# Linear attention and an MLP mixer on one core: from pairs of batches to single batches in a software pipeline

## The chip, the cores and the metric

The kernel runs on one core of a Trainium2 chip. A core has five engines, each with its own instruction queue, worked off in program order: TensorE (PE; its weight loads are shown apart as PEld), VectorE (DVE), ScalarE (ACT), GpSimd (POOL) and SyncE (SP). Here SP only issues transfers. POOL issues the transfers that load weights and cast them to bf16 on the way. Matmuls write to PSUM, which has eight banks of 2 KB a partition; VectorE and ScalarE read it from there.

The metric is the device time of one execution in microseconds, as the median of several runs. Beside it stands one profiled execution, whose trace is read here.

## The reference

For 8 batches, 8 heads, 576 positions and head size 64, a linear attention, then a mixer over positions (tokens) and one over channels:

```python
phi = lambda x: np.where(x > 0, x, np.exp(x) - 1.0) + 1.0
q_p, k_p = phi(q), phi(k)
kv  = einsum('bhsd,bhse->bhde', k_p, v);  z = sum(k_p, axis=2)
num = einsum('bhsd,bhde->bhse', q_p, kv)
den = einsum('bhsd,bhd->bhs', q_p, z)[..., None] + 1e-06
x   = (num / den), heads side by side: (8, 576, 512)
xt  = x.transpose(0, 2, 1)
h   = np.maximum(xt @ w_tok1, 0.0) @ w_tok2       # 576 -> 256 -> 576
u   = x + h.transpose(0, 2, 1)
h2  = np.maximum(u @ w_ch1, 0.0) @ w_ch2          # 512 -> 1536 -> 512
out = u + h2
```

Inputs and output are fp32; the matmuls run in bf16.

## The kernel before

The 576 positions of a batch are four row tiles of 128 (the position is `4p + r`, r = 0 to 3) and a tail of 64. The batches go in four pairs, and the two tails of a pair fill one tile of 128, so that a pair has nine row tiles.

For each batch, in this order:

- **phi** (L114 to L137): a chunk is four heads, 128 x 1024. ScalarE takes exp (L116), VectorE adds 1 (y, L117), takes the minimum of exp and 1 (e, L118), and the maximum of both (L126). The tail has the same steps at half the size (L136).
- **vcast** (L140 to L146): VectorE casts v to bf16 beside a column of ones, which gives z with the same matmul.
- **kv** (L148 to L159): for each of four head pairs, five matmuls of 130 columns (four row tiles and the tail), and ScalarE copies the result to kvbd.
- **qtr** (L161 to L181): TensorE transposes phi(q), ScalarE copies it to qT.
- **nd** (L183 to L200): for each row tile, four matmuls give numerators and denominators in a PSUM tile of two banks, of which there is one buffer. VectorE adds eps (L194), takes the reciprocal (L196) and multiplies (x, L198).
- **mm1** (L203 to L210) and **mm2** (L212 to L223): token mixing. mm1 has two column tiles of five matmuls of 512 columns, evicted with relu by ScalarE. mm2 has two such matmuls for each row tile; VectorE adds x and writes u (L222, and L220 for the tail).
- **utr** (L225 to L233): u transposed into uT.

Then the channel mixing for the pair. **mm3** (L236 to L245) goes over twelve column tiles; each has a group of four matmuls of 512 columns for each of the two batches (L239), evicted with relu by ScalarE (L243), and one of 128 columns for the tails, evicted by VectorE (L245). **mm4** (`slot_4`, L256 to L276) takes nine row tiles, each twelve matmuls of 512 columns in three parts of four, after which VectorE adds u (L266) and SP stores the tile.

The order is written by hand (`manual_schedule`). The first pair starts batch by batch: the whole attention and token mixing of batch 0, mm3 of batch 0 (`slot_a` twelve times), attention and token mixing of batch 1, the rest of mm3. Then, for each pair, the slots of mm3 (24) and mm4 (27) run in order, and a plan puts steps of the next pair behind given slots (`pos`, `ks`, `qs`). phi of k and vcast for the pair after next stand near or behind the last slots, phi of q for the next pair in its first slots.

PSUM has three pools: `ps_big` (three buffers of one bank, for mm3 and mm4), `ps_sm` (three of one bank, for all else) and `ps_nd` (one of two banks). The transfers of the first pair and of the weights are ordered by dependencies on earlier ones (`after`): an instruction waits on its issuing engine until the other transfer has landed, and what stands behind it on that engine waits too. Weights are issued by POOL, all else by SP. w2 is loaded in rows of its own order (w2raw) and rearranged by VectorE (L327, L330).

Of the kernel before, what the change touches and what calls it, by code (L numbers as in the profile page):

```python
# [9 lines left out]
FP32 = mybir.dt.float32  # L10
# [8 lines left out]
def kernel(  # L19
# [30 lines left out]
    work = ctx.enter_context(tc.tile_pool(name="work", bufs=2))  # L50
    outp = ctx.enter_context(tc.tile_pool(name="outp", bufs=3))
    ps_big = ctx.enter_context(tc.tile_pool(name="ps_big", bufs=3, space=bass.MemoryType.PSUM))
    ps_sm = ctx.enter_context(tc.tile_pool(name="ps_sm", bufs=3, space=bass.MemoryType.PSUM))
    ps_nd = ctx.enter_context(tc.tile_pool(name="ps_nd", bufs=1, space=bass.MemoryType.PSUM))
# [30 lines left out]
    u = [const(f"u{i}", [128, 9, DM]) for i in range(2)]  # L85
    uT = const("uT", [128, NDM, 9 * 128])
    cr = const("cr", [128, NCH, 9 * 128])
# [13 lines left out]
    def load_chunk(nm, p, b, g):  # L101
        hs = slice(4 * g, 4 * g + 4)
        s = src[nm][2 * p + b, hs, 0:SM, :].rearrange("h (p r) d -> p h (r d)", r=R)
        return nc.sync.dma_start(out=raw[nm, b][:, hs].rearrange("p h r d -> p h (r d)"), in_=s)
# [8 lines left out]
    def phi_flat(src_flat, dst, n):  # L113
        e = work.tile([128, 1024], BF16, name="e", tag="e")[:, :n]  # L114
        y = work.tile([128, 1024], BF16, name="y", tag="y")[:, :n]
        nc.scalar.activation(out=e, in_=src_flat, func=AF.Exp)  # L116
        nc.vector.tensor_scalar(out=y, in0=src_flat, scalar1=1.0, scalar2=None, op0=ALU.add)  # L117
        nc.vector.tensor_scalar(out=e, in0=e, scalar1=1.0, scalar2=None, op0=ALU.min)  # L118
        dst(e, y)

    def phi(nm, b, g):
        dstt = (kp if nm == "k" else qp)[b]
        f = raw[nm, b][:, 4 * g:4 * g + 4].rearrange("p h r d -> p (h r d)")
# [16 lines left out]
    def vcast(b, g):  # L140
        nc.vector.tensor_copy(out=vs[b][:, :, 4 * g:4 * g + 4, 0:D].transpose([0, 2, 1, 3]),  # L141
                              in_=raw["v", b][:, 4 * g:4 * g + 4])

    def vcast_tail():
        for b in range(2):
            nc.vector.tensor_copy(out=vst[b][half[b], :, 0:D], in_=raw["v", "t"][half[b]])  # L146

    def kv(b, g):  # L148
        ps = ps_sm.tile([128, 2, 256], FP32, name="kv_ps", tag="sm")
        for jj in range(2):  # L150
            j = 2 * g + jj
            for r in range(R):
                nc.tensor.matmul(out=ps[:, jj, 0:2 * D1], lhsT=kp[b][:, r, 2 * j:2 * j + 2, :],  # L153
                                 rhs=vs[b][:, r, 2 * j:2 * j + 2, :], start=(r == 0), stop=False)
            nc.tensor.matmul(out=ps[:, jj, 0:2 * D1], lhsT=kpt[:, 2 * j:2 * j + 2, :],  # L155
                             rhs=vst[b][:, 2 * j:2 * j + 2, :], start=False, stop=True)
        for i in range(2):
            nc.scalar.copy(out=kvbd[b][half[i], 2 * g:2 * g + 2, i * D1:(i + 1) * D1],
                           in_=ps[half[i], :, i * D1:(i + 1) * D1])  # L159

    def qtr(b, g):  # L161
        tp = ps_sm.tile([128, 8, 128], BF16, name="tp", tag="sm")
        for jj in range(2):
            for r in range(R):
                j = 2 * g + jj
                nc.tensor.transpose(  # L166
                    out=tp[:, jj * R + r, :],
                    in_=qp[b][:, r, 2 * j:2 * j + 2, :].rearrange("p a b -> p (a b)"),
                    identity=identity)
        nc.scalar.copy(out=qT[b][:, 2 * g:2 * g + 2].rearrange("p j r c -> p (j r) c"), in_=tp)  # L170

    def qtr_tail():
        tp = ps_sm.tile([128, 8, 128], BF16, name="tp", tag="sm")
# [8 lines left out]
    def nd(b, r):  # L182
        tail = r == R  # L183
        ps = ps_nd.tile([128, 2, 2, 256], FP32, name="nd_ps", tag="nd")
        for j in range(HP):
            nc.tensor.matmul(out=ps[:, j // 2, j % 2, 0:2 * D1],  # L186
# [3 lines left out]
        n = 64 if tail else 128  # L190
        v_ = ps.rearrange("p a b c -> p (a b) c")[ps_, :, 0:2 * D1]
        v_ = v_.rearrange("p j (h e) -> p j h e", h=2)
# [7 lines left out]
            in1=den[:, :, :, None].to_broadcast([n, HP, 2, D]), op=ALU.mult)  # L200


    def mm1(b, mt):  # L203
        ps = ps_sm.tile([128, DM], FP32, name="a_ps", tag="sm")
        ms = slice(128 * mt, 128 * mt + 128)
        for r in range(R):
            nc.tensor.matmul(out=ps, lhsT=w1[:, r, ms], rhs=x[b][:, r, :],  # L207
                             start=(r == 0), stop=False)
        nc.tensor.matmul(out=ps, lhsT=w1t[:, b, ms], rhs=xt, start=False, stop=True)  # L209
        nc.scalar.activation(out=ar[b][:, mt, :], in_=ps, func=AF.Relu)  # L210

    def mm2(p, b, r):  # L212
        tail = r == R
        ps = ps_sm.tile([128, DM], FP32, name="h_ps", tag="sm")
        for kt in range(NT):
            nc.tensor.matmul(out=ps, lhsT=w2t[:, kt, b, :] if tail else w2[:, kt, r, :],  # L216
                             rhs=ar[b][:, kt, :], start=(kt == 0), stop=(kt == NT - 1))
        if tail:
            h = half[b]
            nc.vector.tensor_tensor(out=u[p % 2][h, 8, :], in0=ps[h], in1=xt[h], op=ALU.add)  # L220
        else:
            nc.vector.tensor_tensor(out=u[p % 2][:, 4 * b + r, :], in0=ps, in1=x[b][:, r, :],  # L222
                                    op=ALU.add)  # L223

    def utr(p, t0, n):  # L225
        tp = ps_sm.tile([128, NDM, 2, 128], BF16, name="tp", tag="sm")
        for i in range(n):
            for j in range(NDM):
                nc.tensor.transpose(out=tp[:, j, i, :],  # L229
                                    in_=u[p % 2][:, t0 + i, 128 * j:128 * j + 128],  # L230
                                    identity=identity)
        dst = uT[:, :, 128 * t0:128 * (t0 + n)].rearrange("p j (i c) -> p j i c", i=n)
        nc.scalar.copy(out=dst, in_=tp[:, :, 0:n, :])  # L233


    def mm3_group(mc, c0, n, on_act=True):  # L236
        ps = ps_big.tile([128, 512], FP32, name="c_ps", tag="big")[:, :n]
        for kj in range(NDM):
            nc.tensor.matmul(out=ps, lhsT=wc1[:, kj, 128 * mc:128 * mc + 128],  # L239
                             rhs=uT[:, kj, c0:c0 + n], start=(kj == 0), stop=(kj == NDM - 1))  # L240
        dst = cr[:, mc, c0:c0 + n]
        if on_act:
            nc.scalar.activation(out=dst, in_=ps, func=AF.Relu)  # L243
        else:
            nc.vector.tensor_scalar(out=dst, in0=ps, scalar1=0.0, scalar2=None, op0=ALU.max)  # L245

    def slot_a(mc):
        mm3_group(mc, 0, 512)

    def slot_b(mc):  # L250
        mm3_group(mc, 512, 512)
        mm3_group(mc, 1024, 128, on_act=False)
# [3 lines left out]
    def slot_4(p, t, part):  # L256
        if part == 0:
            held["h2"] = ps_big.tile([128, DM], FP32, name="h2_ps", tag="big")
        ps = held["h2"]
        for kc in range(4 * part, 4 * part + 4):  # L260
            nc.tensor.matmul(out=ps, lhsT=cr[:, kc, 128 * t:128 * t + 128], rhs=wc2[:, kc, :],  # L261
                             start=(kc == 0), stop=(kc == NCH - 1))
# [3 lines left out]
        nc.vector.tensor_tensor(out=o, in0=ps, in1=u[p % 2][:, t, :], op=ALU.add)  # L266
        if t < 8:
            b, r = divmod(t, 4)
# [5 lines left out]


    parts = [(b, g) for b in range(2) for g in range(2)]  # L276
    landed = {}
    for nm, g in (("k", 0), ("v", 0), ("k", 1), ("v", 1)):
        landed[nm, g] = load_chunk(nm, 0, 0, g)
    load_tail("k", 0)  # L280
    load_tail("v", 0)
    landed["q", 0] = load_chunk("q", 0, 0, 0)
    load_chunk("q", 0, 0, 1)
# [4 lines left out]
    after(nc.gpsimd.dma_start(out=w1, in_=moe_w_tok1[0:SM, :].rearrange("(p r) t -> p r t", r=R)),  # L288
          landed["q", 0])
    for b in range(2):  # L290
        nc.gpsimd.dma_start(out=w1t[half[b], b, :], in_=moe_w_tok1[SM:S, :])
    nc.gpsimd.dma_start(out=w2raw, in_=moe_w_tok2.rearrange("(k p) s -> p k s", p=128))
    NB = 4
    CB = DCH // NB
    wc1_in = []
    for i in range(NB):
        cs = slice(CB * i, CB * (i + 1))
        wc1_in.append(nc.gpsimd.dma_start(
            out=wc1[:, :, cs], in_=moe_w_ch1[:, cs].rearrange("(k p) c -> p k c", p=128)))

# [7 lines left out]
    nc.vector.memset(w2t, 0.0)  # L308

    def next_k(b, g):  # L310
        if b == "t":
            phi_tail("k")
            vcast_tail()
        else:
            phi("k", b, g)
            vcast(b, g)

    for g in range(2):
        next_k(0, g)
    next_k("t", 0)  # L320
    kv(0, 0)
    kv(0, 1)
# [3 lines left out]
    for kt in range(NT):  # L326
        nc.vector.tensor_copy(out=w2[:, kt],  # L327
                              in_=w2raw[:, kt, 0:SM].rearrange("k (p r) -> k r p", r=R))
        for b in range(2):
            nc.vector.tensor_copy(out=w2t[:, kt, b, 64 * b:64 * b + 64], in_=w2raw[:, kt, SM:S])  # L330
    qtr(0, 0)
    qtr(0, 1)
# [3 lines left out]
    for mt in range(NT):  # L336
        mm1(0, mt)
    for r in range(R + 1):
        mm2(0, 0, r)
        if r in (2, 4):  # L340
            utr(0, r - 2, 2)

    gate = wc1_in[NB - 2]
    for nm in "kv":
        for g in range(2):
            landed[nm, 1, g] = after(load_chunk(nm, 0, 1, g), gate)
# [166 lines left out]
```

## Time and profile before

| | |
|---|---|
| median of 3 runs | 361.17 us (360.92 to 362.2) |
| the profiled execution | 359.34 us |
| its span, first to last instruction | 357.5 us |
| mean granted TensorE clock | 0.942 |
| TensorE matmul, busy | 280.5 us (78%) |
| TensorE weight loads | 148.2 us (41%) |
| VectorE | 185.4 us (52%) |
| ScalarE | 147.2 us (41%) |
| GpSimd | 10.0 us (3%) |
| read from and written to memory | 35.85 and 9.44 MB |

In the rows that follow, a group of instructions has its line, engine, operation, the tiles that it writes and reads, shapes and count; behind the bar stand its busy time in us, the mean of one in ns, and the idle time of the engine before it, with what ended it. In the timeline, a row starts with its start and its length in us from the start of the span. A row of waits has the waiting instruction, what it waited for, the total in us, how often, and the longest. In the 40 slices, each digit is a tenth of the busy share of 8.9 us, and PEclk is the granted clock in tenths. In a table by stage, the numbers behind the stretch are its length and the busy time of each engine, with the number of instructions in brackets.

### The profile page before, as it was taken

How to read it: one execution, taken by the hardware profiler on the slowest of the kernel's cores; microseconds unless marked ns; L12 is line 12 of the kernel's file. 1: busy time of each engine (PE TensorE's matmuls, PEld its weight loads, DVE VectorE, ACT ScalarE, POOL GpSimd, SP SyncE). 2: the span in 40 equal slices, each digit the busy share in tenths (PEclk: the TensorE clock that was granted, in tenths of full speed). 3: DMA queues.
4: the chain of work that ended last, by engine and by line, in shares of the span. 5: the costliest groups of instructions: out<-in, count | busy, mean ns of one | idle time of the engine just before them, and what ended most of it. 6: DMA issues, size and time to landing. Idle time of an engine off the chain costs nothing.

```text
span 357.5 us, 4635 instructions
## 1 busy us (share of the span) xinstructions
PE 280.5 (78%) x1776; PEld 148.2 (41%) x1776; DVE 185.4 (52%) x406; ACT 147.2 (41%) x229; POOL 10.0 (3%) x19
## 2 busy tenths in 40 slices
PE   0256864389949659808989999939889999999995
PEld 0133423135536324405544455426445454455442
DVE  6574325442599663698575362787571642211221
ACT  3431564135647202556944325239635121366000
POOL 1320300000000000000000000000000000000000
PEclk9999995589987999977999999989999999999999
DMA  7999959940299900169900022110000122100232
GB/s 251 220 180 294 244 152 272 289 109 0 65 297 302 280 29 30 61 202 315 274 2 3 0 61 88 60 61 0 2 0 2 29 88 90 60 0 2 65 114 88
DMA packets 47574, 41.82 MB, mean 117 GB/s; under 512 B 14272, under 2 KB 42816, under 8 KB 47552
## 3 DMA queue, kind: packets, MB, share of 16 engines
q1 hardware_dynamic: 43264, 37.76, 35.9%
q0 software_dynamic: 4288, 3.77, 6.8%
q8 instruction: 14, 0.23, 0.3%
q14 instruction: 8, 0.07, 0.1%
HBM read 35.85 MB, written 9.44 MB: 127 GB/s over the span
## 4 chain that ended last, share of the span: by engine, by line
PE 64%; DVE 23%; ACT 6%; issue 3%; DMA 2%; SPq 1%; ACTq 0%
PE h_ps L261 22%; PE c_ps L239 21%; DVE x L198 6%; PE nd_ps L186 5%; PE a_ps L207 4%; PE h_ps L216 4%; DVE y L117 3%; PE kv_ps L153 3%; DVE vs L141 2%; DMA k_rawt<-in_k_dram 2%; DVE e L118 2%; PE tp L229 2%; DVE kp L126 2%; DVE den L196 2%; ACT e L116 2%
## 5 line engine op out<-in xcount | busy, mean ns | idle before, releaser
L239 PE MATMUL c_ps<-uT,wc 128*128 128x512 bf16 (+1 forms) x576 | 103.8, 330 | 1.7 <-ACT uT L233 1.6
L261 PE MATMUL h_ps<-wc,cr 128*128 128x512 bf16 x432 | 101.8, 381 | 0.0
L243 ACT ACTIVATE cr<-c_ps 128x512 bf16<-128x512 f32 x96 | 57.8, 604 | 49.7 <-PE c_ps L239 49.5
L239 PEld LDWEIGHTS <-wc 128*128 128x128 bf16 x576 | 49.9, 99 | 45.8 <-issue 4.6
L261 PEld LDWEIGHTS <-cr 128*128 128x128 bf16 x432 | 41.3, 98 | 45.7 <-issue 1.2
L266 DVE TENSOR_TENSOR o_sb<-h_ps,u 128x512 f32<-128x512 f32 x36 | 24.8, 690 | 41.7 <-PE h_ps L261 41.7
L245 DVE TENSOR_SCALAR cr<-c_ps 128x128 bf16<-128x128 f32 x48 | 14.0, 291 | 53.4 <-PE c_ps L239 53.4
L233 ACT COPY uT<-tp 128x1024 bf16<-128x1024 bf16 (+1 forms) x20 | 18.2, 928 | 42.1 <-PE tp L229 42.0
L222 DVE TENSOR_TENSOR u<-h_ps,x 128x512 bf16<-128x512 f32 x32 | 21.3, 686 | 20.0 <-PE h_ps L216 19.9
L186 PE MATMUL nd_ps<-kvbd,qT 128*128 128x130 bf16 x128 | 15.1, 244 | 17.0 <-DVE x L198 13.0
L210 ACT ACTIVATE ar<-a_ps 128x512 bf16<-128x512 f32 x16 | 9.6, 597 | 45.4 <-PE a_ps L209 45.4
L118 DVE TENSOR_SCALAR e<-e 128x1024 bf16<-128x1024 bf16 (+1 forms) x40 | 16.0, 401 | 22.5 <-ACT e L116 22.2
L153 PE MATMUL kv_ps<-vs,kp 128*128 128x130 bf16 x128 | 15.2, 270 | 15.5 <-DVE vs L141 15.5
L155 PE MATMUL kv_ps<-vst,kpt 128*128 128x130 bf16 x32 | 8.7, 273 | 23.6 <-DVE vst L146 23.6
L198 DVE TENSOR_TENSOR x<-nd_ps,den 128x512 bf16<-128x512 f32 x32 | 22.1, 691 | 1.1
L116 ACT ACTIVATE e<-k_raw 128x1024 bf16<-128x1024 f32 x16 | 16.5, 1056 | 14.3 <-DVE kp L126 9.2
L153 PEld LDWEIGHTS <-kp 128*128 128x128 bf16 x128 | 12.0, 124 | 19.0 <-DVE kp L126 10.3
L186 PEld LDWEIGHTS <-qT 128*128 128x128 bf16 x128 | 8.6, 106 | 26.2 <-DVE x L198 21.3
L216 PE MATMUL h_ps<-ar,w 128*128 128x512 bf16 x64 | 18.1, 379 | 0.9 <-ACT ar L210 0.9
L116 ACT ACTIVATE e<-q_raw 128x1024 bf16<-128x1024 f32 x16 | 16.6, 1052 | 5.2 <-DVE kp L126 3.9
L170 ACT COPY qT<-tp 128x1024 bf16<-128x1024 bf16 x16 | 16.6, 1035 | 5.1 <-PE tp L166 5.1
L207 PE MATMUL a_ps<-x,w 128*128 128x512 bf16 x64 | 18.5, 416 | 0.0
(55 smaller groups left out, 205.0 us busy)
## 6 DMA issues: line engine op xcount, KB each, us to landing
k_raw<-in_k_dram SPq DMA_DIRECT2D x16, 512.0 KB, 5.2
v_raw<-in_v_dram SPq DMA_DIRECT2D x16, 512.0 KB, 7.0
q_raw<-in_q_dram SPq DMA_DIRECT2D x16, 512.0 KB, 7.9
out_dram<-o_sb SPq DMA_DIRECT2D x32, 256.0 KB, 2.3
wc<-in_moe_w_ch_dram POOLq DMA_DIRECT2D x8, 384.0 KB, 8.0
k_rawt<-in_k_dram SPq DMA_DIRECT2D x8, 128.0 KB, 7.3
v_rawt<-in_v_dram SPq DMA_DIRECT2D x8, 128.0 KB, 6.5
q_rawt<-in_q_dram SPq DMA_DIRECT2D x8, 128.0 KB, 7.4
```

The source lines that it names most:

```text
L116: nc.scalar.activation(out=e, in_=src_flat, func=AF.Exp)
L118: nc.vector.tensor_scalar(out=e, in0=e, scalar1=1.0, scalar2=None, op0=ALU.min)
L153: nc.tensor.matmul(out=ps[:, jj, 0:2 * D1], lhsT=kp[b][:, r, 2 * j:2 * j + 2, :], rhs=vs[b][:, r, 2 * j:2 * j + 2, :], start=(r == 0), sto ...
L186: nc.tensor.matmul(out=ps[:, j // 2, j % 2, 0:2 * D1], lhsT=qTt[b][:, j, :] if tail else qT[b][:, j, r, :], rhs=kvbd[b][:, j, :], start=Tr ...
L198: nc.vector.tensor_tensor(out=dst.rearrange("p (j h d) -> p j h d", j=HP, h=2), in0=v_[:, :, :, 0:D], in1=den[:, :, :, None].to_broadcast( ...
L207: nc.tensor.matmul(out=ps, lhsT=w1[:, r, ms], rhs=x[b][:, r, :], start=(r == 0), stop=False)
L216: nc.tensor.matmul(out=ps, lhsT=w2t[:, kt, b, :] if tail else w2[:, kt, r, :], rhs=ar[b][:, kt, :], start=(kt == 0), stop=(kt == NT - 1))
L222: nc.vector.tensor_tensor(out=u[p % 2][:, 4 * b + r, :], in0=ps, in1=x[b][:, r, :], op=ALU.add)
L239: nc.tensor.matmul(out=ps, lhsT=wc1[:, kj, 128 * mc:128 * mc + 128], rhs=uT[:, kj, c0:c0 + n], start=(kj == 0), stop=(kj == NDM - 1))
L243: nc.scalar.activation(out=dst, in_=ps, func=AF.Relu)
L261: nc.tensor.matmul(out=ps, lhsT=cr[:, kc, 128 * t:128 * t + 128], rhs=wc2[:, kc, :], start=(kc == 0), stop=(kc == NCH - 1))
L266: nc.vector.tensor_tensor(out=o, in0=ps, in1=u[p % 2][:, t, :], op=ALU.add)
```

## The change

The work now goes batch by batch. Stage n runs mm3 of batch n, twelve groups of 512 columns, and part of mm4: a stage of an even batch the four row tiles of that batch, a stage of an odd batch the three tail groups of mm3 and the other five row tiles. Between the groups stand attention and token mixing of batch n+1, one step behind each group (`AT`), and phi and vcast of batch n+2. Stage 0 has mm3 alone and batch 1's phi as well; stage 1 has all nine row tiles of mm4 for the first pair. So batch 1's attention lies between mm3 groups of batch 0.

With it:

- `ps_big` has four buffers of one bank; `ps_sm` has two of two banks, for kv, qtr, nd, mm1, mm2 and utr alike. kv, qtr and mm1 each fill one such tile at once, mm2 and utr take two or four row tiles. `work` has three buffers.
- vcast goes from VectorE to GpSimd, and so do the copies that rearrange w2 and a memset.
- VectorE takes the second half of the copies to qT and uT; the tails of mm3 are gathered four column tiles at a time and evicted by ScalarE.
- The transfers of the start are in another order: k and v of batch 1 directly behind w1, q of batch 1 behind its v, and wc1 and wc2 behind these. GpSimd's copies of w2 stand behind all weight transfers. The loads of batches 2 and 3 wait for the third quarter of wc2; later loads follow the phi that frees their buffer.

```diff
-    work = ctx.enter_context(tc.tile_pool(name="work", bufs=2))
+    work = ctx.enter_context(tc.tile_pool(name="work", bufs=3))
-    ps_big = ... bufs=3    ps_sm = ... bufs=3    ps_nd = ... bufs=1
+    ps_big = ... bufs=4    ps_sm = ... bufs=2
...
+    def vcast(n, g):
+        b = n % 2
+        nc.gpsimd.tensor_copy(out=vs[b][:, :, 4 * g:4 * g + 4, 0:D].transpose([0, 2, 1, 3]),
+                              in_=raw["v", b][:, 4 * g:4 * g + 4])
...
+    def kv(n):
+        ps = ps_sm.tile([128, HP, 256], FP32, name="kv_ps", tag="sm")
+        for j in range(HP):
...
+    def qtr(n):
+        tp = ps_sm.tile([128, HP * R, 128], BF16, name="tp", tag="sm")
...
+        nc.scalar.copy(out=qf[:, 0:8], in_=tp[:, 0:8])
+        nc.vector.tensor_copy(out=qf[:, 8:16], in_=tp[:, 8:16])
...
-        ps = ps_nd.tile([128, 2, 2, 256], FP32, name="nd_ps", tag="nd")
+        ps = ps_sm.tile([128, HP, 256], FP32, name="nd_ps", tag="sm")
...
+    def mm2(n, rs):
+        ps = ps_sm.tile([128, 2, DM], FP32, name="h_ps", tag="sm")
...
+            nc.vector.tensor_tensor(out=u[b][:, rs[0]:rs[0] + len(rs)], in0=ps[:, 0:len(rs)],
+                                    in1=x[b][:, rs[0]:rs[0] + len(rs)], op=ALU.add)
...
+    def utr(n, rs):
+        tp = ps_sm.tile([128, 2, NDM, 2, 128], BF16, name="tp", tag="sm")
...
+            if i == 0:
+                nc.scalar.copy(out=dst, in_=tp[:, i // 2])
+            else:
+                nc.vector.tensor_copy(out=dst, in_=tp[:, i // 2])
...
+    def mm3_tail(i):
+        ps = ps_big.tile([128, 4, 128], FP32, name="c_ps", tag="big")
+        for m in range(4):
...
+        nc.scalar.activation(out=crt[:, 4 * i:4 * i + 4, :], in_=ps, func=AF.Relu)
...
+    def prep_k(n, g):
+        if g == "t":
+            phi_tail("k")
+            vcast_tail()
+        else:
+            phi("k", n, g)
+            vcast(n, g)
+        loads(n + 2, "k", g)
+        loads(n + 2, "v", g)
+    def prep_q(n, g):
+        phi_tail("q") if g == "t" else phi("q", n, g)
+        loads(n + 2, "q", g)
...
+    w_in = after(nc.gpsimd.dma_start(out=w1, ...), landed["q", 0])
...
+    gate = w_in
+    for nm in "kv":
+        for g in range(2):
+            landed[nm, 1, g] = after(load_chunk(nm, 1, g), gate)
+            gate = None
...
+    first_c = after(load_wc1(0), landed["v", 1, 0])
+    landed["q1"] = [after(load_chunk("q", 1, g), landed["v", 1, 1] if g == 0 else None)
+                    for g in range(2)]
+    after(load_wc1(1), landed["q1"][0])
+    for i in range(2, NB):
+        load_wc1(i)
+    last = [load_wc2(i) for i in range(NB)][NB - 2]
+    for kt in range(NT):
+        nc.gpsimd.tensor_copy(out=w2[:, kt], in_=w2raw[:, kt, 0:SM].rearrange(...))
+        for b in range(2):
+            nc.gpsimd.tensor_copy(out=w2t[:, kt, b, 64 * b:64 * b + 64], in_=w2raw[:, kt, SM:S])
...
+    mm1(0)
+    mm2(0, [0, 1])
+    mm2(0, [2, 3])
+    utr(0, [0, 1, 2, 3])
+    mm2(0, [R])
...
+    AT = {"kv": 0, "qt": 1, "qtt": 2, "nd0": 3, "nd1": 4, "nd2": 5, "nd3": 6, "nd4": 7,
+          "mm1": 9, "mm2a": 12, "mm2b": 13, "mm2t": 14, "ut": 15, "utt": 17}
...
+    fill = [(0, lambda: prep_k1(0)), (0, lambda: prep_k1(1)), (2, lambda: phi("q", 1, 0)),
+            (3, lambda: phi("q", 1, 1))]
+    at0 = {"kv": 2, "qt": 5, "nd0": 6, "nd1": 7, "nd2": 8, "nd3": 9, "nd4": 9, "mm1": 11,
+           "mm2a": 11, "mm2b": 11, "mm2t": 11, "ut": 11, "utt": 11}
+    fill += [(at0[nm], fn) for nm, fn in steps(1)]
+    run(m3(0), sorted(fill, key=lambda e: e[0]))
+    first_loads(2)
+    first_loads(3)
+    at1 = {"kv": 23, "qt": 26, "qtt": 27, "nd0": 28, "nd1": 29, "nd2": 30, "nd3": 31, "nd4": 32,
+           "mm1": 34, "mm2a": 36, "mm2b": 37, "mm2t": 38, "ut": 39}
...
+    run(m3(1) + m3t + m4(0, list(range(9))), sorted(fill, key=lambda e: e[0]))
+    for n in range(2, B):
+        p, b = divmod(n, 2)
+        if b == 0:
+            big = m3(n) + m4(p, [0, 1, 2, 3])
+            fill = fill_of(n, AT, [8, 10, 18], [16, 20, 21])
+        else:
+            ts = [4, 5, 6, 7, 8] if n + 1 < B else [8, 4, 5, 6, 7]
+            big = m3(n) + m3t + m4(p, ts)
+            fill = fill_of(n, AT, [8, 10], [18, 22])
+        run(big, fill)
```

`run` puts out the groups in order and behind each the steps whose number it has; `fill_of` gives it the steps of batch n+1 at `at` and phi of batch n+2 (k at `ks`, q at `qs`, the tail last of each).

More of the change, by code (lines that the diff above doesn't have):

```diff
@@ L199, in nd @@
             out=dst.rearrange("p (j h d) -> p j h d", j=HP, h=2), in0=v_[:, :, :, 0:D],
[L200 to L210, printed above, removed]
@@ L221, in mm2 @@
         else:
[L222 to L227, printed above, removed]
-            for j in range(NDM):
[L229 to L233, printed above, removed]
@@ L287 @@
     nc.gpsimd.memset(w1t, 0.0)
[L288 to L299, printed above, removed]
+    nc.gpsimd.memset(w2t, 0.0)
     for b in range(2):
@@ L325 @@
     phi_tail("q")
[L326 to L332, printed above, removed]
+    qtr(0)
     qtr_tail()
```

375 lines of the change are left out of this document (163 added, 212 removed).

## The prediction

> **What bounds the kernel now.** I read first the page's busy shares and its 40 slices.
>
> ```profile
> PE 280.5 (78%) x1776; PEld 148.2 (41%) x1776; DVE 185.4 (52%) x406; ACT 147.2 (41%) x229; POOL 10.0 (3%) x19
> ...
> PE   0256864389949659808989999939889999999995
> PEclk9999995589987999977999999989999999999999
> ```
>
> TensorE is the busiest engine, yet its row has holes at every second or third place up to slice 27, and only the last ten slices are full. The table by stage says where. I cut it at the starts of the stages: first mm3, second mm3 half, and the first mm3 groups of the second and third batch pairs. Columns are length, busy of PE, PEld, DVE, ACT, POOL, the granted clock, DMA share and GB/s.
>
> ```profile
> 0.00:39.38 39.38, 15.16 (x97) 8.95 (x98) 24.87 (x61) 13.51 (x19) 10.02 (x19) 1.00 1.05 242
> 39.38:80.33 40.95, 25.55 (x145) 13.34 (x145) 15.89 (x33) 17.41 (x27) 0.00 (x0) 0.75 0.87 206
> 80.33:163.27 82.94, 60.23 (x411) 33.43 (x411) 55.88 (x119) 36.80 (x53) 0.00 (x0) 0.91 0.48 146
> 163.27:238.94 75.67, 67.44 (x445) 35.83 (x444) 44.93 (x98) 35.62 (x57) 0.00 (x0) 0.97 0.31 91
> 238.94:306.58 67.64, 65.30 (x432) 34.25 (x430) 33.39 (x75) 29.49 (x50) 0.00 (x0) 0.99 0.09 32
> ```
>
> TensorE lacks 24 us in the first stage, 15 in the second, 23 in the third and 8 in the fourth. In none of them is another engine full. The waits of TensorE name the cause:
>
> ```profile
> PE kv_ps L155 <- DVE vst L146: 23.6, 4, 7.7
> PE nd_ps L186 <- DVE x L198: 17.3, 21, 1.3
> PE kv_ps L153 <- DVE vs L141: 15.5, 4, 7.6
> ```
>
> TensorE stands in program order behind kv, which waits for phi and the casts of the same pair, and behind nd, whose single PSUM buffer makes one round trip through VectorE per tile. So the bound is latency of a chain across engines, put ahead of work that is ready.
>
> The full-rate price of that work comes from the end of the chain of waits, where nothing is interleaved:
>
> ```profile
> 306.58 23.50 PE c_ps L239 x144
> 330.08 23.32 PE h_ps L261 x108
> 353.43 0.69 DVE o_sb L266
> ```
>
> 108 matmuls of 512 columns in 23.32 us are 0.216 us each, so 0.864 for a group of four. In the line above, 96 such matmuls take 20.7 us and leave 2.8 for 48 of 128 columns, 0.057 each.
>
> **The change, part by part.** I go along the new program in five terms: the start of the first mm3, batch 1's stage, the groups, the work laid between them, the end.
>
> *Term 1, the first mm3.* Before, the weights w1, w2, wc1 are issued by POOL without a break and VectorE rearranges w2. After, POOL does the rearranging, and these copies stand in its queue behind seven weight transfers, the second of which waits for batch 1's first q chunk. That chunk waits for v of batch 1, and these chunks for w1. mm2 of batch 0 needs the copies. The times are in these rows of the timeline:
>
> ```profile
> 0.74 0.44 SPq L104 DMA_DIRECT2D k_raw<-in_k_dram  x1
> 4.71 0.69 DVE L117 TENSOR_SCALAR y<-k_raw 128x1024 bf16<-128x1024 f32 x1 [0.47 <-DMA k_raw<-in_k_dram]
> 14.61 0.70 POOL L288 DMA_DIRECT2D w<-in_moe_w_tok_dram  x1 [12.84 <-DMA q_raw<-in_q_dram]
> 27.37 0.93 SPq L104 DMA_DIRECT2D k_raw<-in_k_dram  x2
> 34.41 1.24 PE L216 MATMUL h_ps<-ar,w 128*128 128x512 bf16 x5 [0.47 <-ACT ar L210]
> 35.28 3.31 POOL L354 DMA_DIRECT2D wc<-in_moe_w_ch_dram  x4 [15.11 <-DMA v_raw<-in_v_dram]
> 39.38 5.99 PE L239 MATMUL c_ps<-uT,wc 128*128 128x512 bf16 x27 [1.10 <-ACT uT L233]
> ...
> q_raw<-in_q_dram SPq DMA_DIRECT2D x16, 512.0 KB, 7.9
> w<-in_moe_w_tok_dram POOLq DMA_DIRECT2D x1, 256.0 KB, 3.8
> ```
>
> w1 is issued at 14.6, as it still waits for q, and lands 3.8 later: 18.4. Batch 1's k chunks and first v chunk follow; before, they took 7.9 us from the issue (27.37) to POOL's release (35.28): 26.4. The next v chunk adds about 1.7, and q cannot be issued until then: 28.1. A q chunk takes between 4.0 (the first k chunk landed by 4.71, from an issue at 0.74) and the median 7.9; it shares the rings with wc1's first quarter, so I take 5.4: 33.5. Seven more issues at 0.83 (3.31 for four) give 39.3. Then come two copies of 512 elements and four of 64 on POOL.
>
> ```profile
> L287 POOL MEMSET w1t<- 128x512 bf16 x1 | 0.5, 519 | 0.0
> masks.py:199 POOL TENSOR_SCALAR_AFFINE_SELECT identity<-identity 128x128 bf16<-128x128 bf16 x1 | 0.3, 288 | 0.1
> ```
>
> POOL's copy is not in the trace. From below it is the memset (about 1 ns an element), from above the select (about 2.2 with its overhead): 1.0 to 2.9 us for all six, and I take 2.0. mm2 starts at 41.3 instead of 34.4. From there to mm3 it took 5.0 us (34.41 to 39.38). The wider tiles make it longer: two u tiles are now added in one instruction, so the first transposes wait for twice the add, and TensorE comes out of some ten idle microseconds at half clock, as in slices 7 and 8. I take 6.0: **47.3**, which is 8 us later than before. Bounds: 43 (fast q, cheap copies) and 52 (q at its median 7.9 and copies at the upper price).
>
> *Term 2, batch 1's stage* to the first mm3 of batch 1. Before, its attention ran after mm3 of batch 0, alone:
>
> ```profile
> 50.43 1.99 ACT L116 ACTIVATE e<-k_raw 128x1024 bf16<-128x1024 f32 x2
> 80.33 1.02 PE L239 MATMUL c_ps<-uT,wc 128*128 128x512 bf16 x4 [0.47 <-ACT uT L233]
> ...
> 253.12 0.40 PE L186 MATMUL nd_ps<-kvbd,qT 128*128 128x130 bf16 x4
> 253.35 1.02 PE L239 MATMUL c_ps<-uT,wc 128*128 128x512 bf16 x4
> 254.74 0.41 PE L186 MATMUL nd_ps<-kvbd,qT 128*128 128x130 bf16 x4 [0.36 <-DVE x L198]
> ...
> L141 DVE CAST vs<-v_raw 128x1024 bf16<-128x1024 f32 x16 | 11.1, 691 | 0.0
> L194 DVE TENSOR_SCALAR den<-nd_ps 128x8 f32<-128x8 f32 x32 | 5.3, 166 | 16.6 <-PE nd_ps L186 16.6
> L196 DVE RECIPROCAL den<-den 128x8 f32<-128x8 f32 x32 | 6.5, 203 | 1.1
> L198 DVE TENSOR_TENSOR x<-nd_ps,den 128x512 bf16<-128x512 f32 x32 | 22.1, 691 | 1.1
> ```
>
> That chain took 29.9 us. Two nd buffers let VectorE go from tile to tile: 1.06 us of work (the last three rows), 1.13 with its gaps, instead of a round trip of 1.62 (253.12 to 254.74): five tiles save 2.5, more at the half clock. Moving two casts of 0.69 to POOL saves up to 1.4. Against it, twelve mm3 groups (10.4 us) now stand on TensorE inside the chain and their evictions on ScalarE ahead of exp. Most fall in gaps where TensorE would wait for phi and nd; I reckon 2 us of them on the path. I take **28**, with 25 (all hidden) and 33 (half of them on the path).
>
> *Terms 3 and 4, from there on.* What is left is 192 groups at 0.864, 165.8, and twelve tail groups of 16 matmuls of 128 columns, 0.9 each, 10.9: **176.7**. The fill, per batch, at the full clock:
>
> ```profile
> 240.87 0.39 PE L153 MATMUL kv_ps<-vs,kp 128*128 128x130 bf16 x4
> 241.44 1.03 PE L239 MATMUL c_ps<-uT,wc 128*128 128x512 bf16 x4
> 245.38 0.61 PE L166 MATMUL tp<-identity,qp 128*128 128x128 bf16 x8
> 245.83 1.25 PE L239 MATMUL c_ps<-uT,wc 128*128 128x512 bf16 x8
> ```
>
> kv: half in 0.57 (240.87 to 241.44), so 1.13. Eight transposes 0.45 (245.38 to 245.83): q 0.9 and u 0.9, with the tails 0.2. nd: 0.23 (253.12 to 253.35) by five, 1.2. mm1 and mm2: ten times 0.216 each, 4.3. Sum 8.6; six batches **51.8**. The same work before the last stage (306.58 to 353.43) is 181.7 of this 228.5, and the present kernel takes 226.2 for it (80.33 to 306.58): some 45 us are to be had here.
>
> Are they had? A stage of 24 or 30 groups with its fill lasts 29 to 35 us. Each step of the chain has its own groups ahead of it: phi runs 16 groups or more before kv, and nd's 1.13 us on VectorE meets 1.10 on TensorE (0.864 + 0.23), so two buffers carry it. Evictions of 1024 columns (priced as two of x's 0.69) stand against 1.7 us of TensorE per mm2 pair. The loads are issued after phi has freed the buffer, almost a stage ahead of use. VectorE gives up casts and small evictions and takes half of qT's and uT's copies; even with its present 185 us it would be busy 60% of a span of 311, and ScalarE with its 147 under half. I allow **3** us for stalls, between 0 and 14 (two a stage, the price of one late add).
>
> What speaks against it is that POOL's casts run beside phi. Trace: while POOL issues transfers, VectorE's first phi step took 0.98 against the 0.69 above, on an operand of the same shape.
>
> ```profile
> 17.06 3.11 POOL L298 DMA_DIRECT2D wc<-in_moe_w_ch_dram  x4
> 18.14 0.98 DVE L117 TENSOR_SCALAR y<-q_raw 128x1024 bf16<-128x1024 f32 x1
> ```
>
> The Trainium skill, "SBUF — State Buffer", section "SBUF: two separate sides", says that POOL and VectorE share a port pair as an exclusive lock, held for the whole instruction. The stretched 0.98 agrees in direction. By that rule every cast would hold up phi by as much as the cast's own length.
>
> *Term 5, the end*: after the last matmul, an add and a transfer; 353.43 to 357.5, **4.1**, unchanged.
>
> Sum: 47.3 + 28 + 176.7 + 51.8 + 3 + 4.1 = 310.9 us of span. The profiled execution took 359.34 for a span of 357.5, so 1.8 more: 312.7. The median of the runs (361.17) lies 0.5% above the profiled one; the same share gives **314**.
>
> **The rivals.**
>
> *POOL comes early (a).* The wait of mm2 is smaller because q lands fast and POOL's copies cost as little as its memset: 43 instead of 47.3, stage 25, no stalls: 304. For it: the first transfers landed in 4 us. Against: the queue order is fixed, and wc1's first quarter runs beside q.
>
> *The shared port makes VectorE late (b).* If a cast costs 1.0 to 2.2 us (1024 elements by the memset and select prices), the two casts of a batch stretch two phi steps each, up to 4 us a stage in the gap between mm1 and mm2, where VectorE has about 1.5 to spare: 2.5 us by six, less the 3 allowed: +12, and 2 in batch 1's stage: 328. For it: the 0.98. Against: phi is not awaited until the next stage.
>
> *The holes stay (c).* As before, TensorE would wait at each stage's start for phi. A stage now loses about 8 to 15 us a pair (75.67 and 82.94 long, against 63.9 of full-rate work: 54 groups and twice 8.6). With 12 for each of three pairs, 36 more: about 350. Against: phi is laid far ahead.
>
> *Slower (d).* POOL becomes the bound. A stage needs two casts of a chunk and one tail's worth, about three. TensorE's stage is 32 us; to lose the 47 us of gain over six stages a stage would have to last 40, so a cast 13 us. From there the v buffers come free late, SP's queue holds the next loads and the outputs behind them, and the output tiles run out: with 14 us a cast, six stages of 42 instead of 32: 374. For it: no POOL cast of this size is in the trace. Against: it is six times the upper price.
>
> **How the numbers follow.** Forecast 0.52, (a) 0.10, (b) 0.20, (c) 0.14, (d) 0.04. The likeliest time is 314, its own range 305 to 324: the bounds of terms 1 and 2 and of the stalls, not all at one end. The range to hold it 8 times in 10 takes in (a) and (b), 303 to 333, and leaves out (c) and (d). A change of 0.5%, about what this measurement can tell from none, needs (c) at its worst: 0.02. Slower is (d): 0.04. Faster is the rest, 0.94.
>
> **What would show it.** In the changed profile, the first mm3 starts near 47 with TensorE idle some ten microseconds before mm2, waiting for POOL's w2 (term 1; at 39 or less it is wrong). The first mm3 of batch 1 stands near 75. From there TensorE has no hole over 2 us; the wait of nd for x falls from 17.3 us to under 4, and that of kv for v's casts, 39 in all, to under 3 after batch 1. First phi steps far above 0.69, or mm2's adds late, speak for (b); holes at the stage starts for (c); casts above 5 us on POOL for (d). The forecast is wrong if the stages of 54 groups last over 70 us.

## The result and the profile after

The changed kernel takes 319.83 us (319.64 to 321.64, four runs) against 361.05 for the kernel before in the same runs; the ratio is 0.8873 with a 95% interval of 0.8825 to 0.8921. The prediction had 314, with 303 to 333 as its range. The profiled execution took 319.94 us, its span is 318.1.

First the page of the changed kernel, its busy shares and slices of 8 us:

```profile
PE 268.8 (84%) x1745; PEld 143.6 (45%) x1776; DVE 167.2 (53%) x327; ACT 134.7 (42%) x209; POOL 34.4 (11%) x50
...
PE   0236266986999989999999999899999999999994
...
PEclk9999999899999999999999999999999999999999
```

From the eleventh slice on, TensorE's row is full but for two 8s and the last slice, where the kernel before had holes up to its slice 27. TensorE's work is the same (1776 weight loads in both); its busy time falls from 280.5 to 268.8 us, mostly because less of it runs at half clock (mean granted clock 0.994 instead of 0.942). A part of the fall may be the 31 matmuls that this trace lacks (1745 of 1776). What is left open lies in the first eighty microseconds.

The table by stage of the changed kernel, cut at the first mm3, at the first mm3 of batch 1 and behind the last matmul. The columns are length, busy time of PE, PEld, DVE, ACT and POOL, granted clock, DMA share and GB/s:

```profile
0.00:48.61 48.61, 17.47 (x95) 9.17 (x97) 21.82 (x49) 11.07 (x15) 17.37 (x32) 1.00 0.97 213
48.61:77.57 28.96, 22.11 (x142) 11.26 (x144) 16.91 (x34) 15.09 (x23) 5.86 (x6) 0.94 1.01 264
77.57:314.10 236.53, 229.18 (x1508) 123.22 (x1535) 127.80 (x246) 108.51 (x171) 11.19 (x12) 1.00 0.33 100
```

and the same last stretch of the kernel before:

```profile
80.33:353.43 273.10, 239.78 (x1536) 125.94 (x1535) 143.93 (x311) 116.24 (x184) 0.00 (x0) 0.96 0.28 86
```

So the first stretch became 9.2 us longer (39.38 to 48.61), batch 1's stage 12.0 shorter (40.95 to 28.96), the rest 36.6 shorter. Together that is 39.4, the difference of the spans.

The waits of the changed kernel tell what remains. Each row has the waiting instruction, what it waited for, total us, times and the longest:

```profile
DVE qT L176 <- ACT qT L175: 18.4, 8, 4.2
DVE uT L247 <- ACT uT L245: 14.1, 8, 2.2
...
PE kv_ps L157 <- DVE kp L129: 9.8, 3, 7.7
...
PE h_ps L225 <- POOL w L377: 7.4, 2, 7.1
...
PE a_ps L215 <- ACT ar L218: 5.8, 8, 0.7
...
PE nd_ps L193 <- DVE x L204: 1.6, 3, 0.8
```

The wait of nd for x fell from 17.3 us to 1.6, and TensorE's waits for v's casts are gone. What it still waits for phi falls in the first two batches, but for 1.0 us. Two waits are new. mm2 of batch 0 waits for GpSimd's w2, as forecast. And mm1 waits eight times for its own relu, once a batch; the prediction has nothing of it. The first two rows, of the same kind, are VectorE waiting for ScalarE before it copies the other half of a PSUM tile.

### The profile page after: what moved, and what is told of

It reads as the page before. It is cut to its first block, busy times and chain, and to the rows that moved or that the text cites. A ratio compares the mean times of both kernels' runs of the same rounds, so it can differ in the third digit from the quotient of the medians.

```text
span 318.1 us, 4554 instructions
## 1 busy us (share of the span) xinstructions
PE 268.8 (84%) x1745; PEld 143.6 (45%) x1776; DVE 167.2 (53%) x327; ACT 134.7 (42%) x209; POOL 34.4 (11%) x50
## 4 chain that ended last, share of the span: by engine, by line
PE 72%; DMA 8%; DVE 6%; ACT 5%; issue 3%; SPq 3%; POOL 2%; ACTq 0%
PE h_ps L283 28%; PE c_ps L261 23%; PE h_ps L225 5%; DMA q_raw<-in_q_dram 4%; PE c_ps L271 3%; PE a_ps L215 3%; PE nd_ps L193 3%; DMA v_raw<-in_v_dram 3%; PE tp L240 2%; PE tp L170 2%; SPq L112 2%; PE kv_ps L157 2%; ACT ar L218 2%; ACT e L119 1%; DMA w<-in_moe_w_tok_dram 1%
## 5 line engine op out<-in xcount | busy, mean ns | idle before, releaser
L261 PE MATMUL c_ps<-uT,wc 128*128 128x512 bf16 x369 | 91.0, 383 | 4.0 <-DVE uT L247 3.2
L283 PE MATMUL h_ps<-wc,cr 128*128 128x512 bf16 x374 | 87.4, 379 | 0.5
L283 PEld LDWEIGHTS <-cr 128*128 128x128 bf16 x384 | 36.9, 98 | 41.3
L261 PEld LDWEIGHTS <-wc 128*128 128x128 bf16 x384 | 36.2, 99 | 39.8 <-issue 6.0
L231 DVE TENSOR_TENSOR u<-h_ps,x 128x1024 bf16<-128x1024 f32 x16 | 19.4, 1223 | 27.8 <-PE h_ps L225 27.7
L145 POOL CAST vs<-v_raw 128x1024 bf16<-128x1024 f32 x16 | 17.5, 1108 | 85.3 <-PE kv_ps L157 52.8
L245 ACT COPY uT<-tp 128x1024 bf16<-128x1024 bf16 x8 | 8.1, 1012 | 42.3 <-PE tp L240 42.3
L157 PE MATMUL kv_ps<-vs,kp 128*128 128x130 bf16 x128 | 11.2, 231 | 9.8 <-DVE kp L129 9.8
L176 DVE COPY qT<-tp 128x1024 bf16<-128x1024 bf16 x8 | 5.5, 692 | 18.4 <-ACT qT L175 18.4
L157 PEld LDWEIGHTS <-kp 128*128 128x128 bf16 x128 | 9.4, 103 | 11.8 <-DVE kp L129 10.4
L170 PE MATMUL tp<-identity,qp 128*128 128x128 bf16 x128 | 9.9, 231 | 4.8 <-DVE qp L129 4.8
```

Source lines behind the costliest of these rows:

```text
L145: nc.gpsimd.tensor_copy(out=vs[b][:, :, 4 * g:4 * g + 4, 0:D].transpose([0, 2, 1, 3]), in_=raw["v", b][:, 4 * g:4 * g + 4])
L157: nc.tensor.matmul(out=ps[:, j, 0:2 * D1], lhsT=kp[b][:, r, 2 * j:2 * j + 2, :], rhs=vs[b][:, r, 2 * j:2 * j + 2, :], start=(r == 0), stop ...
L231: nc.vector.tensor_tensor(out=u[b][:, rs[0]:rs[0] + len(rs)], in0=ps[:, 0:len(rs)], in1=x[b][:, rs[0]:rs[0] + len(rs)], op=ALU.add)
L283: nc.tensor.matmul(out=ps, lhsT=crt[:, kc, :] if t == 8 else cr[b][:, kc, 128 * r:128 * r + 128], rhs=wc2[:, kc, :], start=(kc == 0), stop ...
```

## The experiments

All ratios are against the kernel before in the same runs. Three theories were to be told apart: queue order (the late w2), tiles guarded as a whole (the new waits), and cover (what makes the gain).

**GpSimd's copies of w2 ahead of the wc1 and wc2 transfers.** The six copies move up; nothing else differs.

```diff
+    for kt in range(NT):
+        nc.gpsimd.tensor_copy(out=w2[:, kt], ...)
+        ...
     first_c = after(load_wc1(0), landed["v", 1, 0])
...
     last = [load_wc2(i) for i in range(NB)][NB - 2]
-    for kt in range(NT):
-        nc.gpsimd.tensor_copy(out=w2[:, kt], ...)
-        ...
```

> GpSimd's copies of w2 stand ahead of all wc1 and wc2 transfers instead of behind them; nothing else differs. Theory (queue order): TensorE's wait for w2 (7.4 us in the trace of the changed kernel) goes, mm2 of batch 0 starts near 35, right behind mm1, and the first mm3 near 42 instead of 48.6: 6 to 7 us shorter, about 313. Rival (transfers): the gated transfers of batch 1 and wc1 set the pace anyway, and what is gained at the first mm3 is lost waiting for q of batch 1 or wc1 within batch 1's stage: 319 to 320.

Measured: 310.71 us (310.11 to 311.56), ratio 0.8628 (0.8604 to 0.8652). Against the changed kernel's ratio that is 9 us, where 6 to 7 were expected. In the changed kernel's timeline (start, length, engine) GpSimd comes to w2 at 40.35, behind a wait for q and seven issues:

```profile
35.11 2.22 POOL L360 DMA_DIRECT2D wc<-in_moe_w_ch_dram  x3 [6.61 <-DMA q_raw<-in_q_dram]
37.30 3.00 POOL L365 DMA_DIRECT2D wc<-in_moe_w_ch_dram  x4
40.35 0.62 POOL L377 COPY w<-w2raw 128x512 bf16<-128x512 bf16 x1
...
41.03 0.61 PE L225 MATMUL h_ps<-ar,w 128*128 128x512 bf16 x1 [7.09 <-POOL w L377]
...
46.82 1.01 ACT L245 COPY uT<-tp 128x1024 bf16<-128x1024 bf16 x1 [12.25 <-PE tp L240]
47.87 0.69 DVE L247 COPY uT<-tp 128x1024 bf16<-128x1024 bf16 x1 [1.76 <-ACT uT L245]
...
48.61 2.75 PE L261 MATMUL c_ps<-uT,wc 128*128 128x512 bf16 x12 [1.40 <-DVE uT L247]
```

With the copies early, as soon as w2raw has landed:

```profile
21.45 0.63 POOL L370 COPY w<-w2raw 128x512 bf16<-128x512 bf16 x1 [4.27 <-DMA w2raw<-in_moe_w_tok_dram]
...
26.52 0.76 POOL L360 DMA_DIRECT2D wc<-in_moe_w_ch_dram  x1 [3.15 <-DMA v_raw<-in_v_dram]
33.06 0.63 PE L225 MATMUL h_ps<-ar,w 128*128 128x512 bf16 x1
...
40.00 2.32 PE L261 MATMUL c_ps<-uT,wc 128*128 128x512 bf16 x10 [1.40 <-DVE uT L247]
```

The first mm3 starts at 40.0 instead of 48.6, and nothing is given back later: the stage of batch 1 takes 28.1 us (29.0 in the changed kernel) and the rest 240.4 of span (240.5). The queue order was nearly the whole of the delay (8.6 of the 9.2 us against the kernel before), and the transfer rival falls.

**mm1's column tiles in two PSUM tiles.**

```diff
-        ps = ps_sm.tile([128, NT, DM], FP32, name="a_ps", tag="sm")
         for mt in range(NT):
+            ps = ps_sm.tile([128, NT, DM], FP32, name="a_ps", tag="sm")
...
-                nc.tensor.matmul(out=ps[:, mt], lhsT=w1[:, r, ms], ...)
+                nc.tensor.matmul(out=ps[:, 0], lhsT=w1[:, r, ms], ...)
```

> mm1's two column tiles go to two PSUM tiles instead of the two halves of one. Theory (a PSUM tile is guarded as a whole): in the changed kernel the second column tile waits for the relu of the first although it lies in another bank, 0.75 us eight times; with two tiles this wait of a_ps for ar falls from 5.8 us to under 1, and the time falls by 4 to 6 us, to about 315. Rival (TensorE is held up by VectorE, not by this): the wait moves to the next step, mm2 for ar or nd's x, and the time stays within 1 us of 319.8.

Measured: 312.81 us (311.53 to 313.23), ratio 0.8689 (0.8666 to 0.8712), some 7 us less than the changed kernel. The wait of mm1 for its relu is gone from the waits. In the changed kernel the last matmul of the first column tile starts at 113.30, and the next one waits for the relu:

```profile
113.30 0.38 PE L217 MATMUL a_ps<-xt,w1t 128*128 128x512 bf16 x1
...
113.78 0.60 ACT L218 ACTIVATE ar<-a_ps 128x512 bf16<-128x512 f32 x1 [6.78 <-PE a_ps L217]
...
114.42 1.02 PE L215 MATMUL a_ps<-x,w 128*128 128x512 bf16 x4 [0.75 <-ACT ar L218]
```

With two tiles the second column tile follows at once (66.22 to 66.44):

```profile
66.22 0.38 PE L217 MATMUL a_ps<-xt,w1t 128*128 128x512 bf16 x1
66.44 1.03 PE L215 MATMUL a_ps<-x,w 128*128 128x512 bf16 x4
```

The hole between starts is 1.12 us instead of 0.22, so 0.9 a batch. Behind the first mm3 of batch 1 the span shrinks by 5.2 us (240.5 to 235.3), about six times that 0.9; batch 1's stage by 1.8. Only half of the 1.8 is the split. The other half lies between the first mm3 and mm1 of batch 1, where the changed kernel's execution had a lower granted clock than this one (the third number from the end, 0.91 and 1.00):

```profile
48.61:67.59 18.98, 15.88 (x102) 8.16 (x104) 12.92 (x29) 11.79 (x18) 3.76 (x4) 0.91 1.15 282
...
47.30:65.36 18.06, 14.48 (x102) 7.72 (x104) 12.91 (x29) 11.57 (x18) 3.28 (x4) 1.00 1.16 277
```

The remaining 1.3 is an earlier first mm3 (47.3), because the transfers landed sooner in this execution; it isn't put down to the edit either. So the split is worth about 6 us of the span. The two column tiles lie in different banks in both kernels, so it isn't the bank that made TensorE wait: the wait comes and goes with the tile. Each of the two tiles is as large as the old one and half used, so that mm1 now takes both buffers of `ps_sm`.

**The transposes in two tiles each**, so that the two halves of the copies are independent.

```diff
-        tp = ps_sm.tile([128, HP * R, 128], BF16, name="tp", tag="sm")
-        for j in range(HP):
+        for i in range(2):
+            tp = ps_sm.tile([128, HP * R, 128], BF16, name="tp", tag="sm")
+            for jj in range(2):
...
+            if i == 0:
+                nc.scalar.copy(out=qf[:, 0:8], in_=tp[:, 0:8])
+            else:
+                nc.vector.tensor_copy(out=qf[:, 8:16], in_=tp[:, 0:8])
```

(and the same in utr; these tiles too are as large as before and half used)

> The transposes of q and of u go to two PSUM tiles each, so that ScalarE's half of the copy does not stand before VectorE's. Theory (a PSUM tile is guarded as a whole): VectorE's waits for ScalarE's half (18.4 and 14.1 us in the changed kernel) shrink to under 5 each. In the middle of the kernel other groups cover them, so the time falls only where nothing covers them, at the first mm3 and the first mm3 of batch 1: about 1 to 1.5 us each, 317 to 318. Rival: the two copies are kept apart by the order of the engines, not by the tile; waits and time stay as they are.

Measured: 315.33 us (314.43 to 316.14), ratio 0.8754 (0.8727 to 0.8781), 4 us less than the changed kernel where 2 to 3 were expected. VectorE now waits for TensorE and no longer for ScalarE before these copies:

```profile
DVE qT L180 <- PE tp L173: 12.1, 6, 3.1
...
DVE uT L252 <- PE tp L245: 6.4, 8, 1.1
```

From the start of mm2 to the first mm3 it takes 6.9 us instead of 7.6, batch 1's stage 27.6 instead of 29.0, and the rest 239.7 instead of 240.5. Those parts are 2.9 us; about 1 more is again an earlier arrival of w2 (40.2 instead of 41.0). The theory holds: the copies were serial because they read one tile.

**The casts of v back on VectorE.**

```diff
-        nc.gpsimd.tensor_copy(out=vs[b][:, :, 4 * g:4 * g + 4, 0:D]..., in_=raw["v", b][...])
+        nc.vector.tensor_copy(out=vs[b][:, :, 4 * g:4 * g + 4, 0:D]..., in_=raw["v", b][...])
```

> The casts of v go back from GpSimd to VectorE; all else is as in the changed kernel. Theory (TensorE bound with slack on the others): VectorE gets 14 us more work, busy 57% instead of 53%, off the path; the maximum of phi, 0.75 us in the mean beside the casts, goes back to 0.69; the time moves by less than 1.5 us, 319 to 321. Rival (the move to GpSimd is a gain of its own): 3 us or more slower, 323 or above. Third (the shared port costs): 2 us or more faster, under 318.

Measured: 320.87 us (319.8 to 320.99), ratio 0.8902 (0.888 to 0.8925); the intervals overlap. The move to GpSimd is worth nothing measurable either way, so neither contention with GpSimd nor the relief of VectorE decides. The run doesn't tell the two apart: they could also cancel.

**The steps in one block.** From batch 2 on all steps of the next batch stand behind the last group of a stage. In this order phi and the cast of the next pair's tails overwrite the tails of k and v before kv of batches 3 and 5 has read them, so these batches compute with wrong tails; the number and the sizes of the instructions are unchanged.

```diff
-            fill = fill_of(n, AT, [8, 10, 18], [16, 20, 21])
+            fill = fill_of(n, {k: 23 for k in AT}, [8, 10, 18], [16, 20, 21])
...
-            fill = fill_of(n, AT, [8, 10], [18, 22])
+            fill = fill_of(n, {k: 29 for k in AT}, [8, 10], [18, 22])
```

> From batch 2 on, attention and token mixing of the next batch stand in one block behind the last group of a stage instead of one step behind each group; phi and its lead are unchanged. Theory (the gain is cover for the chain): the chain kv to uT is then bare, some 15 to 18 us a stage of which 8.6 are work of TensorE, so 7 to 10 us more in each of five stages: 355 to 370, about as slow as the kernel before. Rival (the gain comes from the two nd buffers and phi's lead): under 12 us more in all, below 332.

Measured: 375.21 us, one run; span 373.4. That is 55 us more than the changed kernel, 11 in each of five stages, and more than the kernel before. The page of this run shows the holes and the clock that they cost:

```profile
PE   0254569789999998669986699577996779856995
...
PEclk9999999999999999599995899969998699989999
```

Without the cover the gain is gone, so the rival is out. It came out above the 355 to 370 expected, which had no price for work at half clock around each hole. In the five stages the granted clock was 0.50 for 40.9 us in all, in which TensorE was busy for 29.8; the clock is then some 15 of the 55 us (an estimate: half of that busy time). The other 40, 8 a stage, lie within the 7 to 10 expected for the bare chain.

**phi late.** phi of the batch after next stands behind the last two groups of a stage.

```diff
-            fill = fill_of(n, AT, [8, 10, 18], [16, 20, 21])
+            fill = fill_of(n, AT, [22, 23, 23], [23, 23, 23])
...
-            fill = fill_of(n, AT, [8, 10], [18, 22])
+            fill = fill_of(n, AT, [28, 29], [29, 29])
```

> From batch 2 on, phi of the batch after next stands behind the last two groups of a stage instead of spread from the eighth on; the steps of the next batch are laid as in the changed kernel. Theory: kv, one group later, waits for phi: two chunks are 3.6 us on VectorE and the tail's 1.1, the casts included, less the two groups that cover them; 3 to 5 us in each of four or five stages, and q's phi behind it another 1 to 3: 335 to 360. Rival: in-order TensorE has enough ahead and phi's lead is worth nothing: below 323.

Measured: 333.78 us, one run, just below what was expected; 13.9 us more span. phi moves in four stages, those of batches 2 to 5, so it is 3.5 for each. The waits of TensorE that grew are those for phi:

```profile
PE tp L170 <- DVE qp L129: 11.6, 10, 3.1
PE kv_ps L157 <- DVE kp L129: 11.1, 5, 8.0
PE kv_ps L159 <- DVE kpt L139: 8.8, 3, 4.0
```

In the changed kernel they are 4.8, 9.8 and 5.7, so 11.2 of the 13.9 stand in these rows. phi's lead is needed, but it is the smaller part.

**One buffer for the wide tiles.**

```diff
-    ps_sm = ctx.enter_context(tc.tile_pool(name="ps_sm", bufs=2, space=bass.MemoryType.PSUM))
+    ps_sm = ctx.enter_context(tc.tile_pool(name="ps_sm", bufs=1, space=bass.MemoryType.PSUM))
```

> The PSUM pool of attention and token mixing has one buffer of two banks instead of two. Theory (two buffers carry nd and mm2): every step waits for the eviction of the one before; nd goes back to a round trip of about 1.6 us against 1.10 of TensorE per slot, 0.5 by five, and mm1, mm2 and the transposes lose 0.5 to 1.5 us each: 4 to 8 us a stage, 345 to 375. Rival (a group between two steps is cover enough): under 8 us more, below 328.

Measured: 359.48 us, one run, against 361.11 for the kernel before: without the second buffer nearly the whole gain is lost. The waits of this run:

```profile
PE nd_ps L193 <- DVE x L204: 15.8, 32, 1.2
PE h_ps L225 <- DVE u L231: 10.3, 15, 1.3
```

nd and mm2 go back to one round trip a tile. These two rows are 26.1 us, against 2.1 in the changed kernel; waits for the copies to qT and uT to free the one buffer add 9.0. Together with the block this says that the gain needs both, the order and the second buffer. It doesn't say that the kernel before lacked buffers: it had five banks for the same steps, and this run has two. The new order with the old division of PSUM was not run.

**The three mends together**, with phi of k and the casts of batch 1 ahead of mm1 of batch 0:

```diff
     for r in range(R + 1):
         nd(0, r)
+    prep_k1(0)
+    prep_k1(1)
     mm1(0)
...
-    fill = [(0, lambda: prep_k1(0)), (0, lambda: prep_k1(1)), (2, lambda: phi("q", 1, 0)),
-            (3, lambda: phi("q", 1, 1))]
+    fill = [(0, lambda: phi("q", 1, 0)), (1, lambda: phi("q", 1, 1))]
```

> The early w2 copies, mm1 in two tiles and the halved copies together, and besides phi of k and the casts of batch 1 ahead of mm1 of batch 0, where ScalarE and VectorE stood idle. If the parts add up (6.5 for w2, 5 for mm1, 2.5 for the copies, and 3 to 4 for kv of batch 1 no longer waiting for phi): 302 to 305. If the start is held by transfers: first mm3 still at 46 or later, 310 or more.

Measured: 299.35 us (297.48 to 300.15), ratio 0.8289 (0.8239 to 0.8338), less than the 302 to 305 expected. The first mm3 starts at 37.6, batch 1's stage takes 26.4 us, and from its first mm3 to the last matmul it is 230.3 us, where the prediction counted 228.5 of pure work. kv of batch 1 still waits 2.3 us for casts that stand behind eight weight transfers on GpSimd. That is mended in the last kernel.

**All parts, batch 1's casts early, most of its steps one or two groups earlier.**

```diff
+    vcast(1, 0)
+    vcast(1, 1)
     after(load_wc1(1), landed["q1"][0])
...
-    at0 = {"kv": 2, "qt": 5, "nd0": 6, "nd1": 7, "nd2": 8, "nd3": 9, "nd4": 9, "mm1": 11,
-           "mm2a": 11, "mm2b": 11, "mm2t": 11, "ut": 11, "utt": 11}
+    at0 = {"kv": 0, "qt": 4, "nd0": 5, "nd1": 6, "nd2": 7, "nd3": 8, "nd4": 8, "mm1": 9,
+           "mm2a": 10, "mm2b": 10, "mm2t": 11, "ut": 11, "utt": 11}
```

> As the kernel with all three mends and phi of batch 1's k early, and besides: GpSimd casts batch 1's v right behind its first wc1 transfer instead of behind all eight weight transfers, and batch 1's steps stand two groups earlier among mm3 of batch 0 (kv behind the first group, mm1 behind the tenth, mm2 and the transposes behind the last two). Theory (batch 1's stage is a chain with cover to spare): the wait of kv for v's casts (2.3 us) goes, and the tail of the stage gets two groups of cover; the stage shrinks from 26.4 to 21 to 23 us, 295 to 297 in all. Rival (the stage is bound by q of batch 1 landing near 35 and phi behind it): the stage stays at 25 or more, 299.

Measured: 294.5 us (293.51 to 295.48), ratio 0.817 (0.8143 to 0.8197), a hair under the range expected. It beats both kernels. The stages by the same cuts:

```profile
0.00:37.00 37.00, 15.68 (x95) 8.99 (x97) 26.96 (x55) 13.28 (x17) 15.27 (x29) 1.00 0.89 221
37.00:58.21 21.21, 20.03 (x143) 10.97 (x145) 13.71 (x28) 12.47 (x20) 2.89 (x4) 1.00 1.16 230
58.21:288.40 230.19, 227.98 (x1508) 123.23 (x1535) 128.50 (x246) 109.31 (x172) 17.41 (x18) 1.00 0.41 124
```

Batch 1's stage is 21.2 us with TensorE busy 20.0. Only the first 37 us, in which TensorE waits for the first transfers, phi and nd, still have room.

## Why the prediction was right, point by point

The direction, the size (41 us of 47 forecast) and the mechanism held; the time lies 6 us above the forecast and within its own range of 305 to 324. The span is 7.2 above its sum of 310.9. The signs named in advance came as well: nd's wait fell below 4 us, those for v's casts went, no hole of TensorE behind the start of batch 1's mm3 is over 0.9 us, and the two pairs of stages with 54 groups last 66.4 and 66.1 us (from 124.91 to 191.32 and to 257.40), under the 70 that would have been wrong. By its terms:

*Term 1, the first mm3:* 47.3 forecast, 48.6 measured. mm2 started at 41.0 (41.3 forecast), and that it came so close is partly luck. q landed later (35.1 instead of 33.5), the seven issues were cheaper (5.2 instead of 5.8), and mm2 needed only the first of the six copies to start, 0.6 us where the sum had all six at 2.0 (they took 1.9). Moving the copies alone confirmed the cause. From mm2 to mm3 it took 7.6 instead of 6.0. Here the prediction misread a row: it began mm2 of the kernel before at 34.41, which is its second matmul. The first stands earlier,

```profile
33.56 0.38 PE L216 MATMUL h_ps<-ar,w 128*128 128x512 bf16 x1
```

so the 5.0 it started from was 5.8. Of the rest, 0.7 are the serial copies, as the halved tiles show.

*Term 2, batch 1's stage:* 28 forecast, 29.0 measured. mm1 in two tiles took 0.9 off it, the halved copies 1.4. The parts of the forecast (2.5 for nd, 1.4 for the casts, 2 of mm3 on the path) were not measured apart, so that their sum fits may be luck.

*Terms 3 and 4:* 228.5 of pure work is confirmed by the last two kernels, which need 230 for it. The term that was off in size is the 3 us allowed for stalls: it was 8.0 (236.5). The sentence that two buffers carry the steps was true of nd, whose wait fell to 1.6. But the sum had nothing for two results in the two banks of one tile, as if these were free of each other. mm1 waited for its own relu six times 0.9 us, 5.4 of the 8.0, and the split of mm1 removed 5.2. The other 2.6 are within the 3 allowed.

*Term 5, the end:* 4.0 of 4.1. *From span to median:* 1.8 as forecast for the profiled execution, but the 0.5% added for the median was not there (319.83 against 319.94).

*The rivals.* (a) did not come: q landed late, not fast. (b), the shared port: VectorE is held up beside GpSimd's casts, but it costs nothing that could be measured. In the changed kernel's timeline the first cast and phi's maximum run together, and the maximum takes 1.50 us. With the casts back on VectorE the same one takes 0.69 (last row):

```profile
6.10 1.05 POOL L145 CAST vs<-v_raw 128x1024 bf16<-128x1024 f32 x1 [3.87 <-DMA v_raw<-in_v_dram]
6.20 1.50 DVE L129 TENSOR_TENSOR kp<-e,y 128x1024 bf16<-128x1024 bf16 x1
...
6.76 0.69 DVE L129 TENSOR_TENSOR kp<-e,y 128x1024 bf16<-128x1024 bf16 x1
```

It loses 0.81 us, where 0.95 of the cast was still to come.

The groups of the changed kernel give the mean over all:

```profile
L145 POOL CAST vs<-v_raw 128x1024 bf16<-128x1024 f32 x16 | 17.5, 1108 | 85.3 <-PE kv_ps L157 52.8 <-DMA v_raw<-in_v_dram 32.4
...
L129 DVE TENSOR_TENSOR kp<-e,y 128x1024 bf16<-128x1024 bf16 x16 | 11.9, 743 | 0.6
...
L120 DVE TENSOR_SCALAR y<-k_raw 128x1024 bf16<-128x1024 f32 x16 | 11.0, 686 | 1.8 <-DMA k_raw<-in_k_dram 1.7
```

A cast takes 1.1 us, at the lower end of the 1.0 to 2.2 assumed. In the mean k's maximum lost 0.05 us and its y nothing, so few of the 16 casts can have fallen beside them; the prediction had looked for the loss in y. The Trainium skill, "SBUF — State Buffer", section "Who interferes with whom", says that a VectorE instruction with two SBUF inputs contends with a GpSimd instruction that reads SBUF. The row of the maximum, which has two such inputs, agrees. With the casts back on VectorE the time was the same within its interval, so (b) falls. (c), holes that stay, falls with the full slices; phi placed late shows that they would have come. Its 8 to 15 us lost a pair do not follow from the lengths beside it: 75.67 and 82.94 less 63.9 are 11.8 and 19.0, and the 12 that it went on with is the first of these. (d) needed casts of 13 us.

Not settled: why mm2 of batch 0 starts at times between 38.9 and 41.0 us in kernels whose copies of w2 stand in the same place. In all seven it starts 5.9 us after GpSimd's wait for q ends, so it follows q's landing (33.0 to 35.1 us); what moves that was not tried.

## What to carry to other kernels

Order and buffers only pay together: here the steps put in one block (375 us) and the wide tiles with one buffer (359) each lost the gain. When several results are gathered in one wide PSUM tile, look whether the program makes its waits for the tile or for the part of it; a tile for each result, from the same two buffers, took 0.9 us a batch off TensorE's path. And before compute is moved to an engine that issues transfers, read its queue: six copies of 1.9 us in all cost 9 us behind gated transfers, and ahead of them TensorE did not wait for them at all.

## What the runs showed that was not expected

VectorE's two-input maximum (1.50 instead of 0.69 us beside a GpSimd cast), and not its one-input steps, was held up in the rows above; in the kernel with all three mends, where casts fell on phi of q, the one-input y was hit too, and the casts themselves grew from 1.1 to 1.4 us each:

```profile
40.53 2.78 POOL L145 CAST vs<-v_raw 128x1024 bf16<-128x1024 f32 x2
41.00 1.41 DVE L129 TENSOR_TENSOR qp<-e,y 128x1024 bf16<-128x1024 bf16 x1
...
42.33 1.54 DVE L120 TENSOR_SCALAR y<-q_raw 128x1024 bf16<-128x1024 f32 x1
```

VectorE's copy of a 128 x 1024 bf16 half from PSUM took 0.69 us, as long as the 512 fp32 columns of x, while ScalarE's copy of the same size took 1.01.
